# A planner that keeps pairs of PSUM banks exclusive and allows more time for transfers, and an output product that no longer begins with its direct part

## The chip, the cores and the metric

One NeuronCore of a Trainium2 chip runs the whole kernel. TensorE (PE) does matmuls, VectorE (DVE) and ScalarE (ACT) do element-wise work, SyncE (SP) issues the loads, GpSimd (POOL) issues most stores. The metric is the device time of one execution in microseconds (us); lower is better. Times below are of single executions or the median of several.

## What is computed

Input `x` has 2048 rows (sequence) and 1024 columns. The reference, cut to what matters:

```
a = x @ Wd_re.T ;  b = x @ Wd_im.T              # hidden DFT,   1024 x 1024 each
A = Ws_re @ a - Ws_im @ b                       # sequence DFT, 2048 x 2048 each, real part
h = relu(x @ w1 + b1) ** 2                      # 1024 -> 3584
B = h @ w2 + b2                                 # 3584 -> 1024
g = sigmoid((x * gate_w).sum(-1, keepdims=True))
out = g * A + (1 - g) * B
```

All of it is float32.

## The kernel before

**Precision.** A float32 operand is split into `hi` (the value rounded to fp32r by a ScalarE copy) and `lo` (the rest, a VectorE subtraction). Each product of two 128-row blocks is three matmuls into the same PSUM bank: hi x hi, hi x lo, lo x hi. For narrow operands `hi` and `lo` lie side by side in one block called `both`.

**Stages.** Four stages follow each other without a gap between them: x (the hidden DFT, results `ab`), c (the sequence DFT, results `y`, multiplied by the gate and kept in DRAM as `gy`), h (the first layer in two parts of 2048 and 1536 columns, results `h`), o (the second layer, results `o`). Each stage is a matrix product cut into 2 x 2 quarters and done in seven products in place of eight, from sums and differences of the quarters (the tables `SUMS_L`, `SUMS_R`, `FACTORS`). `seven` runs these in a given order, 1 2 5 6 3 7 4, and says which result each product is added to. A product is either *direct* (`direct`) or is itself cut once more into seven (`twice`, with quarter products 1 6 7 5 2 4 3). In stage o the products are 512 x 1792 by 1792 x 1024, the inner dimension cut into seven steps of 256; `TWICE_O = {1: 2, 2: 3, 3: 3, 4: 3}` says how many pairs of such steps go the second way. Product 4 has three pairs, and one step is left over, done directly. `FIRST_O` says for which products the left-over step comes first: its results are put into new blocks, on top of which the split part is then added; for the others it comes last, after the quarter products.

**Groups and PSUM.** A `Group` is one run of accumulation. It takes one or two of four *pairs of PSUM banks* (a tile `ps` of two rows of 512 columns, one bank each). Row r of the group goes to `ps[r // 2][:, r % 2, :]`. A group that adds to an earlier result starts with a ScalarE copy of that result into PSUM (`onto`; in the profile `ps<-u` or `ps<-o`). When a pair is done, a function takes it up: `put` and `add` write `u`, `o`, `h`, `y` or `ab` blocks, and `final` in stage o does, for each of the two rows, `(ps + b2) * (1 - g)` on VectorE, then adds `gy` (loaded as `raw`) and stores the result from POOL's queue. The last group of the kernel is taken up row by row by `last`, with one pair per row, and stored from the queues of SP and ScalarE.

**The planner.** Nothing is issued while this is recorded. Each instruction becomes an `Op` with the ops it must come after: `Queue.record` compares the parts (`box`) of blocks that they read and write. `plan` then makes the order. Matmuls stand in recorded order and have ideal times `MM` apart; every other op gets a due time backwards from them. A list scheduler with these constants runs through the program: VectorE and ScalarE by size (`VEC`, `ACT`, with ends `VEC_END`, `ACT_END`), DMA issue (`ISSUE`), a latency before and after a transfer (`RING`), a rate (`RATE`) that concurrent queues share in `flow`. On each engine the ready op that is due first goes next. The 55 blocks of 4 KB per partition (`SLOTS`) are handed out in the order of due time less a lead (`LEAD`), by kind: `raw` for loads, `out` for what reads PSUM, `hi` for the rest. `emit` writes the instructions in that order, and each engine keeps it. The framework adds the semaphore waits; those are by what is really used, not by the planner's constants.

Since one line in `emit` issues everything, all instructions of the profile have line L1125, and they are told apart by their tiles.

Of the kernel before, what the change touches and what calls it, by code (L numbers as in the profile page):

```python
# [15 lines left out]
P = 128  # L16
# [2 lines left out]
SLOTS = 55  # L19
WIDE, TALL_C, TALL_O = ((1, 2, 5, 6, 3, 7, 4),) * 3  # L20
TWICE_X, TWICE_C, TWICE_O = (1, 2, 5, 3, 4), {1: 1, 2: 4, 3: 4, 4: 4}, {1: 2, 2: 3, 3: 3, 4: 3}
FIRST_C, FIRST_O = (2,), (2, 4)
WARM = 44
FAR_TALL, FAR_WIDE = ("T2",), ()
TWICE_H = (1, 2, 5, 3, 4), (1, 2, 5, 3, 4)

MM, MM_END, FIRST_MM = 0.2267, 0.18, 6.2
VEC, VEC_END, ACT, ACT_END = (0.086, 1.0417e-3), 0.39, (0.11, 0.89e-3), 0.36
ISSUE, RING, RATE, SEM, LANES = {"sync": 0.36, "scalar": 0.36, "gpsimd": 0.56}, (1.1, 1.1), 400e3, 0.06, 8
LEAD = {"raw": 5.0, "hi": 5.0, "sum": 5.0, "out": 0.0}  # L30

ADD, SUB = ALU.add, ALU.subtract

# [11 lines left out]
def gated_mix_kernel(ctx: ExitStack, tc: tile.TileContext, x4, xn, w4, ct, w1a, w1b, w2, b1, b2, gw, out):  # L45
# [11 lines left out]
    class Sight:  # L57


        def __init__(self, base, chain, box):  # L60
            self.base, self.chain, self.box = base, chain, box
# [12 lines left out]
        def __getattr__(self, name):  # L74
            def later(*args, **kwargs):
                return Sight(self.base, self.chain + (lambda t: getattr(t, name)(*args, **kwargs),), self.box)
            return later
# [21 lines left out]
    class Op:  # L99


        def __init__(self, engine, name, args, kwargs):
            self.engine, self.name, self.args, self.kwargs = engine, name, args, kwargs
            sights = [a for a in (*args, *kwargs.values()) if isinstance(a, Sight)]
            outs = [a for a in (args[0], kwargs.get("accum_out")) if isinstance(a, Sight)]
            self.ins, self.outs = [a for a in sights if not any(a is o for o in outs)], outs
            n = max([a.size() for a in sights] + [0])
            self.load, self.end = 0.0, 0.0
            if name == "dma_start":
                self.time, self.load = ISSUE[engine], n * P * 4 / RATE  # L110
            elif engine == "tensor":
                self.time, self.end = (MM, MM_END) if n >= 512 else (0.13, 0.1)
            elif engine == "scalar":
                self.time, self.end = ACT[0] + ACT[1] * n + (1.3 if args[2] == AF.Sigmoid else 0.0), ACT_END
            elif name == "tensor_scalar":
                self.time, self.end = VEC[0] + VEC[1] * n / 2, VEC_END
            else:
                self.time, self.end = VEC[0] + VEC[1] * n, VEC_END
            self.after, self.then, self.new, self.latest, self.landed = set(), [], [], None, False
# [3 lines left out]
    class Queue:  # L123
# [5 lines left out]
        def __getattr__(self, name):  # L129
            def record(*args, **kwargs):  # L130
                op = Op(self.engine, name, args, kwargs)
                op.latest = urgent[0]
                for sight, write in [(a, False) for a in op.ins] + [(a, True) for a in op.outs]:
                    block = sight.base
                    if not block.seen and block.home in ("slot", "bank"):
                        op.new.append(block)
                    if not block.seen and block.before is not None:
                        op.after.update(o for o, *_ in block.before.seen)
                    for other, box, wrote in block.seen:
                        if (write or wrote or block.home == "bank") and (not box or not sight.box or (  # L140
                                box[0] < sight.box[1] and sight.box[0] < box[1] and (
                                    block.home == "bank" or box[2] < sight.box[3] and sight.box[2] < box[3]))):
                            op.after.add(other)
                    block.seen.append((op, sight.box, write))
                op.after.discard(op)
                ops.append(op)
                return op
            return record
# [168 lines left out]
    class Half:  # L317
# [6 lines left out]
        hi = property(lambda self: self.base.hi[:, :, self.at:self.at + 256])  # L324
# [509 lines left out]
    def c_stage():  # L834
        rows = [Row(n, False) for n in range(2)]
        to = {}

        def target(i, n, k):
            near = Near("y")
            to[near] = i, n, *k  # L840
            return near

        def final(dst, ps):
            i, n, c, rp = to[dst]
            nc.vector.tensor_tensor(dst.slot, dst.slot if ps is None else ps, rows[n].of(c).broadcast_to([P, 2, 512]),
                                    op=ALU.mult)
            rows[n].used()
            stores.append((gy[i, n, c, rp], dst, 0, 2))

        at = len(steps)  # L850
        tall(lambda i, j, q: ab[j, q, i], lambda j, n, q, c: ct[n, c, j, q], 8, TALL_C, TWICE_C, FIRST_C, target, final)
        return at, rows
# [52 lines left out]
    at, rows = c_stage()  # L905
# [5 lines left out]
    at, rows, fetched, ends = o_stage()  # L911
# [31 lines left out]
    ideal, t = [], FIRST_MM  # L943
# [10 lines left out]
    for k, (st, mv, group, also) in enumerate(steps):  # L954
# [13 lines left out]
        mv.used()  # L968
        store_all()
    emit(tc, plan(ops, len(slots), ideal[0]), slots, pools)  # L970


def plan(ops, count, start):

    t = start
# [20 lines left out]
    def lead(op, block):  # L996
        kind = "raw" if op.load else "out" if any(a.base.home == "bank" for a in op.ins) else "hi"
        return op.due - LEAD[kind]

# [10 lines left out]
    moving, at, version = {}, 0.0, 0  # L1010
    lanes = [], []

    def push(t, *what):
        heappush(events, (t, len(events) + 1e-9 * len(order), id(what), what))
# [5 lines left out]
    def loosen(op):  # L1020
        op.wait -= 1
        if not op.wait:
            able(op)

    def hand_out():
        nonlocal head
        while head < len(queue) and free:
# [2 lines left out]
            head += 1  # L1030
            loosen(op)

    def flow(t):
        nonlocal at, version
        for e in moving:
            moving[e][1] -= (t - at) / len(moving)
        at = t
        version += 1
        for e in [e for e in moving if moving[e][1] <= 1e-9]:
            op = moving.pop(e)[0]  # L1040
            push(t + RING[1], "done", op)
        for e, r in rings.items():
            if e not in moving and r:
                op = r.popleft()
                moving[e] = [op, op.load]
        if moving:
            push(t + max(0.0, min(m[1] for m in moving.values())) * len(moving), "flow", version)

    def finish(op):
        op.landed = True  # L1050
# [42 lines left out]
    while events:  # L1093
        now, _, _, what = heappop(events)
        if what[0] == "done":
            finish(what[1])
        elif what[0] == "idle" and not what[1].load:
            for o in what[1].then:
                if o.engine == what[1].engine:
                    loosen(o)  # L1100
        elif what[0] == "ring":
            rings[what[1].engine].append(what[1])
            flow(now)
        elif what[0] == "flow" and what[1] == version:
            flow(now)
        issue(now)
# [60 lines left out]
```

## Time and profile before

| what | value |
|---|---|
| median of 3 runs | 1872.18 us (1870.84 to 1874.9) |
| the profiled execution | 1871.76 us, its span 1869.6 us |
| granted TensorE clock | 0.999 |
| TensorE busy | 1852.4 us (99%), 8162 matmuls |
| VectorE busy | 1761.1 us (94%) |
| ScalarE busy | 1086.2 us (58%) |
| POOL busy | 87.6 us (5%) |
| DMA traffic | 445.04 MB, 238 GB/s over the span |
| a load of 512 KB from issue to landing, median by source | 4.5 to 12.4 us, most 5.5 to 7.3 us |

Rows of the timeline give the start in us from the span's start, the length, engine, line, instruction, `out<-in` by tile names and shape; the bracket at the end is the idle time of the engine just before, and what ended it. An engine name with a q (SPq, ACTq) is its queue, which issues DMAs. Matmuls overlap, so a matmul's length (0.39 us) is more than its step from start to start.

### The profile page before, as it was taken

The page shows a single profiled execution, that of the slowest core. Times are in us where ns is not written, and L with a number is a line of the kernel's source. Part 1 is how long each engine was busy: PE and PEld are TensorE (multiplying, and loading weights), DVE is VectorE, ACT ScalarE, POOL GpSimd, SP SyncE. Part 2 cuts the span into 40 slices and gives each one's busy share as a digit, 9 for nine tenths or more (in the row PEclk, how much of TensorE's full clock was granted, in tenths as well). Part 3 has the DMA queues.
Part 4 walks back from the last instruction along what each step waited for, and adds up shares of the span by engine and source line. Part 5 has one row for each costly group of instructions (what it writes and reads, how often), then busy time and mean ns, then how long its engine had stood idle before and what let it go on. Part 6 is the DMA issues. An engine that isn't in the chain of part 4 may idle for free. (4 is left out here: it accounts for less than half of the span.)

```text
span 1869.6 us, 22164 instructions
## 1 busy us (share of the span) xinstructions
PE 1852.4 (99%) x8162; PEld 1529.5 (82%) x8162; DVE 1761.1 (94%) x1728; ACT 1086.2 (58%) x1231; POOL 87.6 (5%) x162
## 2 busy tenths in 40 slices
PE   9999999999999999999999999999999999999998
PEld 7888888888888888888888888788887888887887
DVE  8997998999889899999997999999999998989988
ACT  6474554563343554466584798767977435364462
POOL 0000100000000000000000001000010000000000
PEclk9999999999999999999999999999999999999999
DMA  4641979449798379444551845737664798649952
GB/s 180 259 169 67 352 264 385 159 152 409 266 324 324 136 268 411 158 166 168 219 198 56 333 170 184 270 122 284 240 240 172 288 386 317 269 146 380 363 180 90
DMA packets 128860, 445.04 MB, mean 238 GB/s; under 512 B 14176, under 2 KB 23664, under 8 KB 128752
## 3 DMA queue, kind: packets, MB, share of 16 engines
q1 hardware_dynamic: 106848, 365.10, 53.1%
q0 software_dynamic: 21616, 78.14, 10.6%
q8 instruction: 64, 1.05, 0.2%
q10 hardware_dynamic: 288, 0.39, 0.1%
q14 instruction: 44, 0.36, 0.1%
HBM read 364.92 MB, written 78.65 MB: 237 GB/s over the span
## 5 line engine op out<-in xcount | busy, mean ns | idle before, releaser
L1125 PE MATMUL ps<-hi 128*128 128x512 f32 x2034 | 793.5, 391 | 6.5 <-DVE h L1125 2.6
L1125 PE MATMUL ps<-hi,lo 128*128 128x512 f32 x2034 | 792.9, 390 | 1.7 <-DVE o L1125 1.7
L1125 PE MATMUL ps<-lo,hi 128*128 128x512 f32 x2034 | 792.4, 390 | 0.0
L1125 ACT ACTIVATE hi<-raw 128x1024 fp32r<-128x1024 f32 (+2 forms) x384 | 394.2, 1037 | 341.7 <-DVE raw L1125 212.1
L1125 DVE TENSOR_TENSOR lo<-raw,hi 128x1024 fp32r<-128x1024 f32 (+2 forms) x384 | 454.1, 1200 | 13.4 <-ACT hi L1125 10.7
L1125 PEld LDWEIGHTS ps<-hi 128*128 128x128 f32 x2034 | 382.5, 188 | 88.9 <-ACT hi L1125 4.0
L1125 PEld LDWEIGHTS ps<-hi,lo 128*128 128x128 f32 x2034 | 382.5, 188 | 82.7 <-DVE o L1125 2.6
L1125 PEld LDWEIGHTS ps<-lo,hi 128*128 128x128 f32 x2034 | 382.5, 188 | 79.5 <-DVE lo L1125 0.2
L1125 PE MATMUL ps<-hi,both 128*128 128x512 f32 x1344 | 416.1, 390 | 2.5 <-ACT ps L1125 2.5
L1125 DVE TENSOR_TENSOR raw<-raw 128x1024 f32<-128x1024 f32 (+1 forms) x276 | 327.6, 1209 | 28.1 <-DMA raw<-in_ct 11.7
L1125 ACT ACTIVATE hi<-sum 128x1024 fp32r<-128x1024 f32 x216 | 219.6, 1034 | 157.5 <-DVE sum L1125 111.0
L1125 PEld LDWEIGHTS ps<-hi,both 128*128 128x128 f32 x1344 | 252.3, 188 | 56.1 <-ACT ps L1125 3.8
L1125 DVE TENSOR_TENSOR lo<-sum,hi 128x1024 fp32r<-128x1024 f32 (+1 forms) x216 | 255.1, 1198 | 13.5 <-PE ps L1125 7.4
L1125 PE MATMUL ps<-lo,both 128*128 128x512 f32 x672 | 261.7, 389 | 0.0
L1125 DVE TENSOR_TENSOR sum<-raw 128x1024 f32<-128x1024 f32 (+2 forms) x156 | 160.9, 1041 | 8.3 <-PE ps L1125 4.4
L1125 ACT ACTIVATE u<-ps 128x1024 f32<-128x1024 f32 (+1 forms) x116 | 112.2, 972 | 71.4 <-PE ps L1125 53.6
L1125 PEld LDWEIGHTS ps<-lo,both 128*128 128x128 f32 x672 | 126.2, 188 | 26.0
L1125 DVE TENSOR_TENSOR sum<-raw,sum 128x1024 f32<-128x1024 f32 (+2 forms) x117 | 128.7, 1103 | 7.2 <-PE ps L1125 6.1
L1125 DVE TENSOR_TENSOR h<-h,ps 128x1024 f32<-128x1024 f32 (+1 forms) x92 | 98.7, 1085 | 8.7 <-ACT u L1125 6.2
L1125 ACT ACTIVATE ps<-u 128x1024 f32<-128x1024 f32 (+1 forms) x84 | 82.1, 980 | 29.2 <-DVE o L1125 7.4
L1125 ACT ACTIVATE both<-sum 128x512 fp32r<-128x512 f32 x96 | 59.3, 626 | 66.0 <-DVE sum L1125 54.0
L1125 ACT ACTIVATE h<-h,b1c 128x512 f32<-128x512 f32 x112 | 75.7, 710 | 10.0 <-DVE h L1125 9.9
(47 smaller groups left out, 731.5 us busy)
## 6 DMA issues: line engine op xcount, KB each, us to landing
raw<-in_ct SPq DMA_DIRECT2D x153, 512.0 KB, 6.7
raw<-h SPq DMA_DIRECT2D x134, 512.0 KB, 7.3
raw<-in_x SPq DMA_DIRECT2D x107, 512.0 KB, 5.5
raw<-in_w SPq DMA_DIRECT2D x98, 512.0 KB, 7.1
raw<-ab SPq DMA_DIRECT2D x72, 512.0 KB, 7.1
h<-h POOLq DMA_DIRECT2D x48, 512.0 KB, 5.3
raw<-in_w1a SPq DMA_DIRECT2D x36, 512.0 KB, 6.2
ab<-ab POOLq DMA_DIRECT2D x32, 512.0 KB, 7.0
```

What stands on the lines that cost most here:

```text
L1125: made = getattr(real[op.engine], op.name)(*(actual(a) for a in op.args), **{k: actual(v) for k, v in op.kwargs.items()})
```

## The change

Four things change. The order of dependences in `Queue.record`: before, two accesses to a pair of banks depend on each other if they touch the same row of the pair; after, always, reads beside reads included. The planner's costs: ScalarE's cost per element falls and its end rises; the latencies of a transfer go from 1.1 + 1.1 to 1.6 + 2.0 us; the rate is 405 GB/s for one queue alone and 370 GB/s shared by several. The lead of loads goes from 5 to 9 us. And `FIRST_O` loses product 4, the last of stage o and of the kernel: its left-over step comes at the end, so the kernel's last group is the left-over step of one quarter (12 matmuls) and no longer a quarter product of 36.

```
-FIRST_C, FIRST_O = (2,), (2, 4)
+FIRST_C, FIRST_O = (2,), (2,)
...
-VEC, VEC_END, ACT, ACT_END = (0.086, 1.0417e-3), 0.39, (0.11, 0.89e-3), 0.36
-ISSUE, RING, RATE, SEM, LANES = {"sync": 0.36, "scalar": 0.36, "gpsimd": 0.56}, (1.1, 1.1), 400e3, 0.06, 8
-LEAD = {"raw": 5.0, "hi": 5.0, "sum": 5.0, "out": 0.0}
+VEC, VEC_END, ACT, ACT_END = (0.086, 1.0417e-3), 0.39, (0.11, 0.84e-3), 0.41
+ISSUE, RING, RATE, SEM, LANES = {"sync": 0.36, "scalar": 0.36, "gpsimd": 0.56}, (1.6, 2.0), (405e3, 370e3), 0.06, 8
+LEAD = {"raw": 9.0, "hi": 5.0, "sum": 5.0, "out": 0.0}
...
-                self.time, self.load = ISSUE[engine], n * P * 4 / RATE
+                self.time, self.load = ISSUE[engine], n * P * 4 / RATE[0]
...
-                        if (write or wrote or block.home == "bank") and (not box or not sight.box or (
-                                box[0] < sight.box[1] and sight.box[0] < box[1] and (
-                                    block.home == "bank" or box[2] < sight.box[3] and sight.box[2] < box[3]))):
+                        if block.home == "bank" or (write or wrote) and (not box or not sight.box or (
+                                box[0] < sight.box[1] and sight.box[0] < box[1] and box[2] < sight.box[3]
+                                and sight.box[2] < box[3])):
...
+    def share():
+        return 1.0 if len(moving) == 1 else len(moving) * RATE[0] / RATE[1]
+
     def flow(t):
...
-            moving[e][1] -= (t - at) / len(moving)
+            moving[e][1] -= (t - at) / share()
...
-            push(t + max(0.0, min(m[1] for m in moving.values())) * len(moving), "flow", version)
+            push(t + max(0.0, min(m[1] for m in moving.values())) * share(), "flow", version)
```

In the built program, all engines but ScalarE have as many instructions as before; ScalarE has seven fewer (copies between PSUM and `o` or `u` in product 4). TensorE's order is the same up to the first matmul of product 4. On the other engines the order differs from the first microseconds on.

## The prediction

> **What bounds the kernel now.** I read the page first, then the waits of TensorE (engine, tile, what it waited for: us in total, times, longest), then the timeline around each of those waits.
>
> ```profile
> span 1869.6 us, 22164 instructions
> PE 1852.4 (99%) x8162; PEld 1529.5 (82%) x8162; DVE 1761.1 (94%) x1728; ACT 1086.2 (58%) x1231; POOL 87.6 (5%) x162
> PEclk9999999999999999999999999999999999999999
> ...
> PE ps L1125 <- DVE h L1125: 2.6, 2, 1.8
> PE ps L1125 <- ACT ps L1125: 2.5, 3, 1.4
> PE ps L1125 <- DVE o L1125: 2.5, 3, 0.8
> PE ps L1125 <- ACT hi L1125: 1.8, 2, 1.2
> PE ps L1125 <- DVE u L1125: 1.1, 1, 1.1
> PE ps L1125 <- DVE ones L1125: 1.1, 1, 1.1
> ```
>
> TensorE is the bound, at full clock, so the matmuls themselves are out of reach of this change. What can move is the 11.6 us of waits, the tail behind the last matmul, and waits that do not exist yet. The waits for `hi` and `ones` belong to the start, which keeps its first loads and matmuls. The other nine are these, with two rows that give the pace (start, length, instruction, then idle time and who ended it):
>
> ```profile
> 1704.21 0.39 PE L1125 MATMUL ps<-lo,both 128*128 128x512 f32 x1
> ...
> 1706.93 0.39 PE L1125 MATMUL ps<-lo,hi 128*128 128x512 f32 x1
> 1708.16 0.50 PE L1125 MATMUL ps<-hi,lo 128*128 128x512 f32 x1 [0.85 <-DVE o L1125]
> 1708.50 0.39 PE L1125 MATMUL ps<-hi 128*128 128x512 f32 x1
> ...
> 1711.57 0.51 PE L1125 MATMUL ps<-hi 128*128 128x512 f32 x1 [0.84 <-DVE o L1125]
> ...
> 1715.25 0.51 PE L1125 MATMUL ps<-hi,lo 128*128 128x512 f32 x1 [0.84 <-DVE o L1125]
> ```
>
> ```profile
> 1166.42 0.50 PE L1125 MATMUL ps<-hi 128*128 128x512 f32 x1 [1.11 <-DVE u L1125]
> ...
> 1197.03 0.47 PE L1125 MATMUL ps<-hi 128*128 128x512 f32 x1 [1.76 <-DVE h L1125]
> ...
> 1226.65 0.47 PE L1125 MATMUL ps<-hi 128*128 128x512 f32 x1 [0.82 <-DVE h L1125]
> ...
> 1409.08 0.50 PE L1125 MATMUL ps<-hi,both 128*128 128x512 f32 x1 [0.60 <-ACT ps L1125]
> ...
> 1413.47 0.50 PE L1125 MATMUL ps<-hi,both 128*128 128x512 f32 x1 [1.37 <-ACT ps L1125]
> ...
> 1842.16 0.50 PE L1125 MATMUL ps<-hi,both 128*128 128x512 f32 x1 [0.57 <-ACT ps L1125]
> ```
>
> From 1704.21 to 1706.93 stand 12 steps: 0.227 us each. At 1708.16 the step took 1.23 and the next one 0.34 (to 1708.50), so 1.12 us were lost where the row shows 0.85 idle. I add that 0.27 to each idle time: lost are 3 x 1.11 = 3.3 us at 1708 to 1715, 1.4 + 2.0 + 1.1 = 4.5 at 1166 to 1227, 0.9 + 1.6 = 2.5 at 1409 and 1413, 0.8 at 1842. In all 11.1 us; no planner can gain more inside the stream.
>
> **The change, part by part.** The sum is made against the profiled execution, 1871.76 us: span 1869.6 and 2.2 around it. The median of the runs, 1872.18, lies 0.4 above.
>
> *Exclusive pairs.* The waits at 1708 to 1715 are for these:
>
> ```profile
> 1707.35 0.75 DVE L1125 SCALAR_TENSOR_TENSOR o<-ps,b2c,g 128x512 f32<-128x512 f32 x1 [0.23 <-PE ps L1125]
> ...
> 1710.76 0.75 DVE L1125 SCALAR_TENSOR_TENSOR o<-ps,b2c,g 128x512 f32<-128x512 f32 x1 [0.86 <-PE ps L1125]
> ...
> 1714.44 0.75 DVE L1125 SCALAR_TENSOR_TENSOR o<-ps,b2c,g 128x512 f32<-128x512 f32 x1 [1.11 <-PE ps L1125]
> ```
>
> Each reads row 0 of a pair while matmuls of row 1 remain: the old planner put the reader between them (1, 3 and 4 matmuls of the pair stand behind it in program order). The next matmul starts 0.05 to 0.06 us after the reader ends in all three (1708.10 to 1708.16, 1711.51 to 1711.57, 1715.19 to 1715.25): the program's own wait holds it, though it writes the other bank. In the changed order no matmul of a pair stands behind such a reader, so all three waits go: -3.3. What is late next is the reader, by the remaining matmuls (at most 4 x 0.227 = 0.9), and nobody but an output store waits for it. No other instruction's dependences change but those of matmuls, which run in one fixed order anyway, so this edit does no more. The Trainium skill (PSUM — Partial Sum Buffer, in the summary of rules for kernel authors) says that a read of PSUM beside running matmuls should target a different bank. This is that case: by it the pair needs no exclusive treatment, the edit buys nothing, and the sum below would be -1.5 in place of -4.8. The trace shows the wait in this case all the same, 0.84 to 0.85 us idle each time.
>
> *ScalarE's costs and the time for transfers.* They change no instruction; they change the order on VectorE, ScalarE, POOL and SP, and which block a load gets. Loads get their block with 9 us in hand instead of 5, so they displace `hi` and `sum` blocks. Through the order I followed three places.
>
> At 1409 and 1413 the copies into PSUM were late because VectorE came late to `u`, having idled behind ScalarE:
>
> ```profile
> 1370.39 1.23 DVE L1125 TENSOR_TENSOR lo<-sum,hi 128x1024 fp32r<-128x1024 f32 x1 [2.22 <-ACT hi L1125]
> ...
> 1372.57 0.69 DVE L1125 TENSOR_TENSOR both<-sum,both 128x512 fp32r<-128x512 f32 x1 [0.94 <-ACT both L1125]
> ...
> 1368.70 0.71 ACT L1125 ACTIVATE h<-h,b1c 128x512 f32<-128x512 f32 x1
> ...
> 1370.27 0.71 ACT L1125 ACTIVATE h<-h,b1c 128x512 f32<-128x512 f32 x1
> ```
>
> Those `h` activations, nobody's need, stand some 33 places earlier in the new order. That removes part of VectorE's 2.22 + 0.94 = 3.2 us idle; I take half, 1.6, of a possible 2.5: -1.6.
>
> At 1166 to 1227 VectorE had no rest but two waits for loads, 0.85 + 1.81 = 2.7 us:
>
> ```profile
> 1165.15 1.22 DVE L1125 TENSOR_TENSOR u<-u,ps 128x1024 f32<-128x1024 f32 x1
> ...
> 1172.96 1.23 DVE L1125 TENSOR_TENSOR raw<-raw 128x1024 f32<-128x1024 f32 x1 [0.85 <-DMA raw<-in_x]
> ...
> 1177.73 1.23 DVE L1125 TENSOR_TENSOR raw<-raw 128x1024 f32<-128x1024 f32 x1 [1.81 <-DMA raw<-in_x]
> ...
> 1165.11 1.92 SPq L1125 DMA_DIRECT2D raw<-in_x  x4
> ...
> 1156.76 0.39 PE L1125 MATMUL ps<-hi,lo 128*128 128x512 f32 x1
> ```
>
> In the changed order these four loads keep their place on SP but go into blocks whose last matmul is the one at 1156.76, so they can start 8 us sooner; the second landed 7.8 us after the burst began, hence now near 1164.7. The first `raw<-raw` moves nine places forward, ahead of the `u` addition at 1165.15 that TensorE waits for. Less work stands before both by one 768-wide instruction (0.86), so VectorE reaches the load at 1165.15 - 0.86 - 1.14 = 1163.15 and waits 1.5: 0.6 worse there. Before the `h` additions at 1197 and 1227 one more instruction (1.14, or 0.86) stands. Together 2.7 - 0.6 - 1.1 = 1.0: -1.0, between -4.5 (all gone) and +9 (below).
>
> *Product 4 without its direct part first.* No matmul is added; seven ScalarE copies of about 1 us go, off the path. Its 48 direct matmuls (48 x 0.227 = 10.9 us) move from the head of the product to its end. Two things follow. First, the split operands are due 10.9 us sooner. In the windows view of tile `both`, which only the twice split products use (window, us, busy and count by engine):
>
> ```profile
> core 0: us, PE busy (x) PEld busy (x) DVE busy (x) ACT busy (x), PEclk, DMA share, GB/s
> 1716.00:1796.00 80.00, 0.00 (x0) 0.00 (x0) 3.44 (x5) 3.15 (x5) 1.00 0.78 308
> ```
>
> VectorE has made five of them before 1796 and TensorE has used none, so VectorE is ahead by more than one such step. I take 0; without that cover TensorE would stand up to 10.9. Second, the wait at 1842: the group that takes up the last quarter product was second in line and is now third, 12 matmuls or 2.7 us later against 0.57 missing: -0.8.
>
> *The tail.* Before, the last group had 36 matmuls and VectorE was idle before its two rows. Now the last four groups end 12 matmuls (2.72 us) apart, three of them with a whole final.
>
> ```profile
> 1855.04 1.40 DVE L1125 SCALAR_TENSOR_TENSOR o<-ps,b2c,g 128x512 f32<-128x512 f32 x2
> 1856.48 1.22 DVE L1125 TENSOR_TENSOR o<-o,raw 128x1024 f32<-128x1024 f32 x1
> 1857.62 1.40 DVE L1125 SCALAR_TENSOR_TENSOR o<-ps,b2c,g 128x512 f32<-128x512 f32 x2
> ...
> 1862.89 0.75 DVE L1125 SCALAR_TENSOR_TENSOR o<-ps,b2c,g 128x512 f32<-128x512 f32 x1 [2.62 <-PE ps L1125]
> 1863.68 0.69 DVE L1125 TENSOR_TENSOR o<-o,raw 128x512 f32<-128x512 f32 x1
> 1863.83 0.39 PE L1125 MATMUL ps<-hi,both 128*128 128x512 f32 x1
> 1864.29 0.74 DVE L1125 SCALAR_TENSOR_TENSOR o<-ps,b2c,g 128x512 f32<-128x512 f32 x1
> 1865.07 0.69 DVE L1125 TENSOR_TENSOR o<-o,raw 128x512 f32<-128x512 f32 x1
> 1865.79 0.35 ACTq L1125 DMA_DIRECT2D out<-o  x1
> ```
>
> A final takes 2.58 (1855.04 to 1857.62), so the third, begun 2.65 before the last matmul's end, frees VectorE 0.07 before it. Then come both rows, 2.87 (1862.89 to 1865.07, and 0.69): 2.8 us after the last matmul, where it was 1.54 (1864.22 to 1865.76). +1.3; from 0 to +2.6, one final more, if VectorE brings a backlog. The POOL store of the third final starts with the last rows and has less behind it than the last ScalarE store.
>
> *Unseen.* Much of VectorE's queue of 1,728 instructions stands in another order. A wait costs 1.24 on average (11.1 by nine); I take half a new one, +0.6.
>
> Sum: -3.3 - 1.6 - 1.0 - 0.8 + 1.3 + 0.6 = -4.8, so 1867.0 for such an execution and, with the 0.4, **1867.4** for the median.
>
> **Rivals.**
>
> *Loads at the head of the queue (slower).* If the four loads still landed near 1172.9, `u` would start behind `raw<-raw` at 1172.96 + 1.14 = 1174.10, not 1165.15: TensorE stands 9.0 us longer. With -1.0 taken out, the rest is -3.8; the kernel is slower once that wait adds 3.8, that is when they land after 1167.8. At 9.0 the time is 1877.4. For it: VectorE's instructions start in the order of its queue, and the new order puts such reads ahead. Against: the block is free 8 us sooner.
>
> *More is won.* The loads come early enough, no wait is new: -3.3 - 4.5 - 2.5 - 0.8 + 1.3 = -9.8, 1862.4. For it: VectorE and ScalarE idle before loads in many places; against: VectorE stays full from 1180 to 1227.
>
> *The waits only move.* Three new ones more, 3.7: 1871.1. For it: VectorE is 94% busy, and any order leaves some addition late.
>
> *Pairs were not the cause.* The three waits stay: 1867.4 + 3.3 = 1870.7. Against: three times a matmul starts 0.05 us after the reader. The Trainium skill's rule of the different bank, above, would have it this way.
>
> **How the numbers follow.** The forecast has 0.50 (its own range 1864.5 to 1870), loads at the head 0.11, more won 0.17, moved waits 0.13, pairs 0.04, other losses, such as `hi` and `sum` starved of blocks, 0.05. A measurement of this kernel tells about 0.2%, 3.7 us, from no change: faster is below 1868.4, slower above 1875.9. Three quarters of the forecast and all of "more" are faster, 0.55; the rest of the forecast, the moved waits and the pairs give 0.29; 0.16 is slower. The range leaves out the far half of "more" and the slower cases: 1862 to 1874.5.
>
> **What would show it.** No wait for `DVE o` between 1700 and 1720; no `DVE o` reader between matmuls of its pair. The first `raw<-raw` near 1163, waiting under 2 us, and total TensorE waits near 5 us. The last VectorE addition 2.8 us behind the last matmul. Wrong would be a wait above 3 us on an addition behind `raw<-raw`, or a `both` matmul waiting for `lo` or `both` right after product 7.

## The result

| | before | after |
|---|---|---|
| median of 9 runs each | 1872.1 us (1870.64 to 1874.9) | 1867.4 us (1867.18 to 1868.57) |
| ratio, 95% interval | 1 | 0.9975 (0.9965 to 0.9985) |
| the profiled execution | 1871.76 us, span 1869.6 | 1867.58 us, span 1865.3 |

The changed kernel is faster by 0.25%, 4.7 us, where 1867.4 was forecast. First the page of the profile after (span, busy times, clock) and its waits of TensorE, the same two views as before (the line of `emit` is L1128 in this kernel):

```profile
span 1865.3 us, 22218 instructions
PE 1850.1 (99%) x8162; PEld 1528.2 (82%) x8162; DVE 1760.2 (94%) x1728; ACT 1075.9 (58%) x1224; POOL 87.9 (5%) x162
PEclk9999999999999999999999999999999999999999
...
PE ps L1128 <- ACT hi L1128: 3.1, 2, 2.2
PE ps L1128 <- DVE h L1128: 2.6, 4, 0.9
PE ps L1128 <- DVE lo L1128: 1.3, 2, 1.1
PE ps L1128 <- DVE ones L1128: 1.1, 1, 1.1
PE ps L1128 <- DVE u L1128: 0.5, 1, 0.5
```

The shares of busy time hardly move: TensorE is still 99% busy, VectorE 94%. What to see is which names are gone. `DVE o` (2.5 us, the three readers) and `ACT ps` (2.5 us, the copies at 1409, 1413 and 1842) have no row any more; `DVE lo` is new. `ACT hi` has grown from 1.8 to 3.1 us, all of it in the start, which as a whole is only 0.2 us later. The rows with idle time on TensorE's timeline after, outside the start:

```profile
100.12 0.50 PE L1128 MATMUL ps<-hi,lo 128*128 128x512 f32 x1 [1.11 <-DVE lo L1128]
...
1139.67 0.50 PE L1128 MATMUL ps<-hi 128*128 128x512 f32 x1 [0.34 <-DVE h L1128]
...
1167.69 0.50 PE L1128 MATMUL ps<-hi 128*128 128x512 f32 x1 [0.48 <-DVE u L1128]
...
1197.45 0.47 PE L1128 MATMUL ps<-hi 128*128 128x512 f32 x1 [0.87 <-DVE h L1128]
...
1226.82 0.47 PE L1128 MATMUL ps<-hi 128*128 128x512 f32 x1 [0.56 <-DVE h L1128]
...
1350.68 0.47 PE L1128 MATMUL ps<-hi 128*128 128x512 f32 x1 [0.85 <-DVE h L1128]
```

Matmuls stand in the same order in both kernels up to product 4, so the start of the n-th matmul can be held against the start of the n-th before. The table has the lead that it gains (minus) or loses from place to place, in us. The measured rows, each rounded, come to -4.0; before rounding they come to -4.2, all that lies between the two spans (4.3 from the rounded ones):

| place (us) | forecast | measured |
|---|---|---|
| start | 0 | +0.2 |
| 98, `lo` late | | +1.2 |
| 284 | | -0.4 |
| 1136 to 1140 | | +1.0 |
| 1166 to 1227 | -1.0 | -1.7 |
| 1350 | | +0.8 |
| 1409 and 1413 | -1.6 | -2.6 |
| 1708 to 1715, the readers | -3.3 | -3.5 |
| product 4, where the wait at 1842 was | -0.8 | -0.2 (-0.9 there, +0.6 at 1825 and 1829) |
| behind the last matmul | +1.3 | +1.2 |
| unseen | +0.6 | (the four rows without a forecast: +2.6) |
| sum | -4.8 | -4.0 |

The tail on VectorE's timeline after, with the stores that follow:

```profile
1856.15 1.41 DVE L1128 SCALAR_TENSOR_TENSOR o<-ps,b2c,g 128x512 f32<-128x512 f32 x2
1857.60 1.23 DVE L1128 TENSOR_TENSOR o<-o,raw 128x1024 f32<-128x1024 f32 x1
1858.74 0.74 DVE L1128 SCALAR_TENSOR_TENSOR o<-ps,b2c,g 128x512 f32<-128x512 f32 x1
1859.24 0.72 POOL L1128 DMA_DIRECT2D out<-o  x1 [2.01 <-DVE o L1128]
1859.52 0.69 DVE L1128 TENSOR_TENSOR o<-o,raw 128x512 f32<-128x512 f32 x1
1860.13 0.74 DVE L1128 SCALAR_TENSOR_TENSOR o<-ps,b2c,g 128x512 f32<-128x512 f32 x1
1860.24 0.34 SPq L1128 DMA_DIRECT2D out<-o  x1
1860.91 0.69 DVE L1128 TENSOR_TENSOR o<-o,raw 128x512 f32<-128x512 f32 x1
1861.63 0.35 ACTq L1128 DMA_DIRECT2D out<-o  x1
```

The last matmul ended at 1858.83; VectorE has no gap from the third final on and ends at 1861.60, 2.8 us later, where it was 1.5 before.

### The profile page after: what moved, and what is told of

The parts are those of the page before. It is cut to its first block, busy times and chain, and to the rows that moved or that the text cites. A ratio compares the mean times of both kernels' runs of the same rounds, so it can differ in the third digit from the quotient of the medians.

```text
span 1865.3 us, 22218 instructions
## 1 busy us (share of the span) xinstructions
PE 1850.1 (99%) x8162; PEld 1528.2 (82%) x8162; DVE 1760.2 (94%) x1728; ACT 1075.9 (58%) x1224; POOL 87.9 (5%) x162
## 4 chain that ended last, share of the span: by engine, by line
PE 84%; ACT 7%; DVE 6%; issue 2%; DMA 1%; SPq 0%; ACTq 0%; DVEq 0%
PE ps L1128 84%; ACT h L1128 3%; ACT hi L1128 3%; DVE lo L1128 2%; DVE h L1128 1%; DVE sum L1128 1%; ACT u L1128 1%; DVE raw L1128 1%; DMA raw<-in_x 1%; ACT ps L1128 0%; DVE o L1128 0%; DMA raw<-in_w 0%; DVE ab L1128 0%; DVE u L1128 0%; SPq L1128 0%
## 5 line engine op out<-in xcount | busy, mean ns | idle before, releaser
L1128 PE MATMUL ps<-hi 128*128 128x512 f32 x2034 | 792.2, 390 | 6.3 <-ACT hi L1128 3.1
L1128 PE MATMUL ps<-hi,lo 128*128 128x512 f32 x2034 | 791.2, 389 | 1.3 <-DVE lo L1128 1.3
L1128 PE MATMUL ps<-lo,hi 128*128 128x512 f32 x2034 | 790.9, 389 | 0.0
L1128 ACT ACTIVATE hi<-raw 128x1024 fp32r<-128x1024 f32 (+2 forms) x384 | 392.7, 1035 | 322.5 <-DVE raw L1128 183.9
L1128 DVE TENSOR_TENSOR lo<-raw,hi 128x1024 fp32r<-128x1024 f32 (+2 forms) x384 | 451.7, 1195 | 15.7 <-ACT hi L1128 10.7
L1128 PEld LDWEIGHTS ps<-hi 128*128 128x128 f32 x2034 | 382.2, 188 | 88.7 <-ACT hi L1128 3.7
L1128 PEld LDWEIGHTS ps<-hi,lo 128*128 128x128 f32 x2034 | 381.9, 188 | 81.7 <-DVE lo L1128 2.2
L1128 PEld LDWEIGHTS ps<-lo,hi 128*128 128x128 f32 x2034 | 382.0, 188 | 79.6 <-DVE lo L1128 0.4
L1128 PE MATMUL ps<-hi,both 128*128 128x512 f32 x1344 | 415.2, 389 | 0.1
L1128 DVE TENSOR_TENSOR raw<-raw 128x1024 f32<-128x1024 f32 (+1 forms) x276 | 324.3, 1203 | 8.6 <-DMA raw<-in_ct 6.3
L1128 ACT ACTIVATE hi<-sum 128x1024 fp32r<-128x1024 f32 x216 | 220.7, 1034 | 180.2 <-DVE sum L1128 121.7
L1128 PEld LDWEIGHTS ps<-hi,both 128*128 128x128 f32 x1344 | 252.2, 188 | 53.2 <-DVE both L1128 0.5
L1128 DVE TENSOR_TENSOR lo<-sum,hi 128x1024 fp32r<-128x1024 f32 (+1 forms) x216 | 254.8, 1195 | 14.5 <-PE ps L1128 12.0
L1128 PE MATMUL ps<-lo,both 128*128 128x512 f32 x672 | 261.4, 389 | 0.0
L1128 DVE TENSOR_TENSOR sum<-raw 128x1024 f32<-128x1024 f32 (+2 forms) x156 | 160.8, 1038 | 17.2 <-PE ps L1128 14.7
L1128 ACT ACTIVATE u<-ps 128x1024 f32<-128x1024 f32 (+1 forms) x116 | 112.4, 972 | 79.9 <-PE ps L1128 62.4
L1128 PEld LDWEIGHTS ps<-lo,both 128*128 128x128 f32 x672 | 126.1, 188 | 26.1
L1128 DVE TENSOR_TENSOR sum<-raw,sum 128x1024 f32<-128x1024 f32 (+2 forms) x117 | 128.4, 1099 | 1.9 <-PE ps L1128 0.6
L1128 DVE TENSOR_TENSOR h<-h,ps 128x1024 f32<-128x1024 f32 (+1 forms) x92 | 98.2, 1081 | 7.4 <-ACT u L1128 5.9
L1128 ACT ACTIVATE both<-sum 128x512 fp32r<-128x512 f32 x96 | 58.7, 623 | 69.9 <-DVE sum L1128 48.9
L1128 ACT ACTIVATE ps<-u 128x1024 f32<-128x1024 f32 (+1 forms) x80 | 78.0, 977 | 23.9 <-DVE u L1128 5.8
L1128 ACT ACTIVATE h<-h,b1c 128x512 f32<-128x512 f32 x112 | 76.1, 710 | 11.2 <-DVE h L1128 11.2
```

Of the source, the lines that this page charges most:

```text
L1128: made = getattr(real[op.engine], op.name)(*(actual(a) for a in op.args), **{k: actual(v) for k, v in op.kwargs.items()})
```

## The experiments

The parts were put in and taken out one at a time. Ratios are each against runs of the kernel before beside it, so that they can be held against each other; a median is of that kernel's own runs.

| kernel | pairs | product 4 | transfers | lead 9 | ScalarE costs | median us | ratio (95%) |
|---|---|---|---|---|---|---|---|
| after | new | new | new | new | new | 1867.4 | 0.9975 (0.9965 to 0.9985) |
| e1 | new | old | old | old | old | 1868.9 | 0.9983 (0.9974 to 0.9992) |
| e2 | old | new | old | old | old | 1874.6 | 1.0012 (1.0003 to 1.0021) |
| e3 | new | old | new | new | new | 1865.6 | 0.9967 (0.9955 to 0.9979) |
| e4 | old | new | new | new | new | 1873.8 | 1.0007 (0.9999 to 1.0016) |
| e5 | new | old | new | old | old | 1863.2 | 0.9947 (0.9935 to 0.9959) |
| e6 | new | old | old | new | old | 1866.0 | 0.9962 (0.9949 to 0.9974) |
| e7 | new | old | old | old | new | 1867.3 | 0.9968 (0.9957 to 0.9980) |
| e8 | new | old | new | new | old | 1863.0 | 0.9947 (0.9933 to 0.9960) |
| e9 | new | new | new | new | old | 1864.0 | 0.9950 (0.9937 to 0.9962) |
| e10 | new | old | longer still | new | old | 1863.8 | 0.9949 (0.9936 to 0.9963) |

### Pairs and product 4

**e1**, only the dependence rule changed:

```
-                        if (write or wrote or block.home == "bank") and (not box or not sight.box or (
...
+                        if block.home == "bank" or (write or wrote) and (not box or not sight.box or (
```

> The kernel before with exclusive pairs as the only change. Theory: the three waits at 1708 to 1715 us (0.85 + 0.84 + 0.84 us idle, 3.3 us with the slow steps) come from readers placed between the matmuls of their pair; in this order no matmul of a pair stands behind such a reader, the rest of the order is the old one, so 1872.1 - 3.3 = 1868.8 us, and the other six waits stay within 0.3 us each. Rival (the pair is not the cause, the additions were just late): the waits stay, 1872.1 us.

Measured: 0.9983, 3.2 us. The three waits are gone and the lead jumps by 3.5 us at that place, as expected. The six other waits did not stay within 0.3 us: at 1166 the idle time grew from 1.11 to 1.68, at 1409 the wait of 0.60 was gone, at 1413 it fell from 1.37 to 0.85, and 0.9 us was lost at 1135 to 1138, though VectorE's order up to these places is the old one. So from one execution of the same order to another, such places differ by half a microsecond and more, 1409 and 1413 together by 1.4. The theory stands, the rival falls.

**e2**, only product 4:

```
-FIRST_C, FIRST_O = (2,), (2, 4)
+FIRST_C, FIRST_O = (2,), (2,)
```

> The kernel before with product 4 without its direct part first as the only change. Theory: in this order six readers, not three, stand between matmuls of their pair (three new ones in the last 10 us, where the left-over steps end row by row), so +3.3 us, -0.8 for the wait at 1842, +1.2 for the tail: 1872.1 + 3.7 = 1875.8 us. Rival (the two parts of the change do not need each other): +1.2 - 0.8 only, 1872.5 us.

Measured: 1.0012, 2.2 us slower, where 3.7 were expected and the rival had 0.4. On TensorE's timeline of e2 near its end:

```profile
1853.97 0.50 PE L1125 MATMUL ps<-hi,lo 128*128 128x512 f32 x1 [0.84 <-DVE o L1125]
...
1858.10 0.50 PE L1125 MATMUL ps<-hi 128*128 128x512 f32 x1 [0.84 <-DVE o L1125]
...
1862.00 0.50 PE L1125 MATMUL ps<-hi 128*128 128x512 f32 x1 [0.84 <-DVE o L1125]
```

The three new waits are there, each exactly as long as those at 1708 to 1715. The wait at 1842 is gone. What is missing is 0.7 us of the tail (5.9 us behind the last matmul, not 6.5: the waits space the last finals out, so VectorE has no queue there) and a net 1.2 us that this execution gained ahead of product 4, 1.7 of it won at 1409 and 1413, where nothing had been changed.

**e3**, the changed kernel with the old `FIRST_O`:

> The changed kernel with the direct part of product 4 first again. Theory: the new order of product 4 cost more than it gave: the tail behind the last matmul goes from 6.5 back to 5.3 us (-1.2), the short waits at 1825 and 1829 (0.6 lost) go, the wait at 1842 (0.8) may return: 1867.4 - 1.0 = 1866.4 us. Rival (the new order of product 4 is part of the gain): 1867.4 + 0.8 or more, 1868.2 us and above.

Measured: 0.9967 in place of 0.9975. The intervals overlap, so by the times alone it is no proof; the profiles show the place. From before product 4 (where e3 leads by 6.5 us and the changed kernel by 5.1) to the last matmul e3 loses 0.3 and the changed kernel wins 0.2, but behind the last matmul it is 4.95 against 6.50 us. The rest of the 2.4 us between their spans, 1.4 us, arose ahead of product 4, 1.3 of it within the first 15 us, where two executions differ in their first loads. e8 and e9 below also differ in product 4 alone and say the same: e8 loses 0.3 and e9 wins 0.2 up to the last matmul, and behind it they take 4.94 and 6.49 us. So in both pairs of profiles the new product 4 costs 1.0 us.

**e4**, the changed kernel with the old dependence rule:

> The changed kernel without exclusive pairs. Theory: six readers stand between matmuls of their pair, each makes the next matmul wait 1.1 us with its slow step: 1867.4 + 6.7 = 1874.1 us, with six waits for DVE o of 0.8 us idle. Rival (with the new costs of ScalarE and of transfers the readers come late enough anyway): 1867.4 us.

Measured: 1.0007 in place of 0.9975, 6.0 us, with six waits for `DVE o`, 5.1 us idle in all:

```profile
PE ps L1128 <- DVE o L1128: 5.1, 6, 0.8
```

So the rule for pairs is worth 3.2 us to the old kernel and 6.0 to the new one: without it the three readers that the new product 4 adds cost 3.5 us on TensorE's timeline.

### The planner's costs

**e5**, **e6**, **e7**: each on top of e1. The edits are the lines of the diff for `RING`, `RATE` and `share` (e5), for `LEAD` (e6), for `ACT` and `ACT_END` (e7).

> Exclusive pairs and, of the costs, the transfer latencies and rates alone (lead 5, old ScalarE costs, product 4 as before); to be held against exclusive pairs alone, 1868.9 us. Pairs with all three costs took 1865.6, so 3.3 us are to be shared out. Theory (loads that start earlier take away VectorE's waits for loads and with them TensorE's waits at 1165 to 1227 and 1409): loads become startable 0.6 to 1.2 us earlier against their use, about a third of what all three give, so -1 us, 1867.9; VectorE's waits for loads fall from 30 us to about 23. Rival (any reshuffle gives about a microsecond either way): 1867.9 to 1869.9 with no relation to the waits for loads.

> Exclusive pairs and the lead of 9 us for loads alone; against 1868.9. Theory: loads become startable 2 to 2.7 us earlier, most of what all three give, so -2.2 us, 1866.7; VectorE's waits for loads fall from 30 us to about 15. At 1197 to 1227 two more VectorE instructions stand ahead of the h additions, which can cost 1 us. Rival (reshuffle): 1867.9 to 1869.9.

> Exclusive pairs and the new ScalarE costs alone; against 1868.9. Theory: no load starts earlier, so the waits for loads stay near 30 us and the time is 1868.9 within 0.8 us. Rival (reshuffle): as much as the other two, 1867.9 to 1869.9; or all of the 3.3 us if ScalarE's order was the cause of the waits at 1409: 1866.

Measured: e5 0.9947, e6 0.9962, e7 0.9968, against 0.9983 of e1. The waits of VectorE for transfers (loads, in e6 also 3.2 us for stores), summed over their rows, are 33.1 us before, 29.9 in e1, 22.0 in e5, 23.0 in e6, 28.6 in e7, 10.5 in the changed kernel. That half of the theory holds for e5 and e7, where it forecast 23 and 30; for e6 it forecast 15. The other half does not hold: e5 wins far more than its share, and e6 less than e5 though both shorten the waits alike. The rival does no better, since all three medians lie below its 1867.9. So the sum of the waits for loads does not tell the time; single places do, where the order of a queue has changed. The lead of matmul n over the kernel before, in profiled executions, names the places:

| place (us) | e1 | e5 | e6 | e7 | after |
|---|---|---|---|---|---|
| 98 | 0.0 | 0.0 | 0.0 | +1.1 | +1.2 |
| 1135 to 1140 | +0.9 | 0.0 | 0.0 | +0.7 | +1.0 |
| 1166 to 1227 | +0.2 | -1.6 | -0.8 | -0.9 | -1.7 |
| 1350 | 0.0 | 0.0 | 0.0 | +1.1 | +0.8 |
| 1409 and 1413 | -1.4 | -2.6 | -0.5 | -2.6 | -2.6 |

At 1409 and 1413 the question is why ScalarE keeps VectorE waiting. The prediction named four `h` activations that nobody needs. In the built orders of the kernel before, e1 and e6 they stand at places 941 to 951 of ScalarE's queue, around the `hi` copy that VectorE waits for (944); in e7 and in the changed kernel all four, in e5 three of them, stand at 908 to 917. VectorE's timeline in e6:

```profile
1368.28 1.22 DVE L1125 TENSOR_TENSOR lo<-sum,hi 128x1024 fp32r<-128x1024 f32 x1 [1.38 <-ACT hi L1125]
...
1370.46 0.69 DVE L1125 TENSOR_TENSOR both<-sum,both 128x512 fp32r<-128x512 f32 x1 [0.95 <-ACT both L1125]
```

and the same two instructions in the changed kernel, with no idle time ahead of them:

```profile
1369.05 1.22 DVE L1128 TENSOR_TENSOR lo<-sum,hi 128x1024 fp32r<-128x1024 f32 x1
1370.19 0.69 DVE L1128 TENSOR_TENSOR both<-sum,both 128x512 fp32r<-128x512 f32 x1
```

But in e8 and e9 (below) the four stand at 943 to 951 again, around the same copy, and TensorE does not wait. What the four kernels with a wait share is another row of ScalarE, two or three instructions ahead of that copy: a `hi<-raw` that waits for a store of `h` to land. ScalarE's timeline before, and in e8 (the last row of each cut is the copy):

```profile
1366.79 1.06 ACT L1125 ACTIVATE hi<-raw 128x1024 fp32r<-128x1024 f32 x1 [2.41 <-DMA h<-h]
1367.76 1.04 ACT L1125 ACTIVATE hi<-sum 128x1024 fp32r<-128x1024 f32 x1
1368.70 0.71 ACT L1125 ACTIVATE h<-h,b1c 128x512 f32<-128x512 f32 x1
1369.32 1.05 ACT L1125 ACTIVATE hi<-sum 128x1024 fp32r<-128x1024 f32 x1
```

```profile
1359.86 1.06 ACT L1128 ACTIVATE hi<-raw 128x1024 fp32r<-128x1024 f32 x1
1360.83 1.04 ACT L1128 ACTIVATE hi<-sum 128x1024 fp32r<-128x1024 f32 x1
1361.78 0.71 ACT L1128 ACTIVATE h<-h,b1c 128x512 f32<-128x512 f32 x1
1362.39 1.05 ACT L1128 ACTIVATE hi<-sum 128x1024 fp32r<-128x1024 f32 x1
```

This wait is 2.41 us before, 1.74 in e1, 1.41 in e2, 2.19 in e6; of the other eight kernels only e9 has it (1.21 us, ended at 1361.31), and there VectorE idles 0.18 us behind it. So the activations in their old place do no harm without that wait. Whether moving them away would be enough while the wait stays, no run shows. The wait also differs between executions: e1 and e2, with VectorE's old order up to here, lose 1.2 and 0.9 us at 1409 and 1413 where the profiled execution of the kernel before lost 2.6.

TensorE then waits 1.76 us at 1411.69 in e6, 0.85 at 1412.70 in e1, 0.60 at 1412.34 in e2, and not at all in the changed kernel, e3 to e5 and e7 to e10.

The waits at 98 and 1350 are there in the kernels with the new ScalarE costs and in no other. That is why e7 wins little by its profile (span 1865.8 against 1865.4 in e1): it gains 1.2 us more than e1 at 1409 and loses 2.2 at 98 and 1350.

**e8**, the first two costs together, and **e9**, the changed kernel with the old ScalarE costs:

```
-VEC, VEC_END, ACT, ACT_END = (0.086, 1.0417e-3), 0.39, (0.11, 0.84e-3), 0.41
+VEC, VEC_END, ACT, ACT_END = (0.086, 1.0417e-3), 0.39, (0.11, 0.89e-3), 0.36
```

> Exclusive pairs, transfer costs and lead, without the new ScalarE costs; against 1865.6 for all three. Theory: loads start as early as with all three, so 1865.6 within 0.8 us, and VectorE's waits for loads stay near 11 us. Rival (the ScalarE costs carry a part): 1866.6 or more.

> The changed kernel with the old ScalarE costs. Theory: the new ScalarE costs put one VectorE addition ahead at 98 and one at 1350 us, each makes TensorE wait about 0.9 to 1.1 us idle (those waits are there in all kernels with the new costs, and in none without); without them 1867.4 - 2.2 = 1865.2 us, and no wait for DVE lo at 98. Rival (they came with the longer transfers or the lead): 1867.4.

Measured: e8 0.9947 where all three costs gave 0.9967 (e3), so leaving the ScalarE costs out wins 3.7 us more by the ratios, 2.2 by the spans (the intervals overlap a little); neither theory nor rival had that sign. e9 was made to test it on the whole change: 0.9950 in place of 0.9975, 4.7 us by the ratios, 3.2 by the spans (1862.1 against 1865.3), where 2.2 were expected. Its waits of TensorE:

```profile
PE ps L1128 <- ACT hi L1128: 3.1, 2, 2.3
PE ps L1128 <- DVE h L1128: 1.5, 2, 0.9
PE ps L1128 <- DVE ones L1128: 1.1, 1, 1.1
PE ps L1128 <- DVE lo L1128: 0.2, 1, 0.2
```

The 1.1 us for `DVE lo` are gone and two of four `DVE h`. The mechanism at 98 is the place of one VectorE addition some 20 us earlier. In the changed kernel and in e8:

```profile
79.56 1.22 DVE L1128 TENSOR_TENSOR ab<-ab,ps 128x1024 f32<-128x1024 f32 x1
80.69 1.22 DVE L1128 TENSOR_TENSOR sum<-raw 128x1024 f32<-128x1024 f32 x1
...
97.71 3.49 DVE L1128 TENSOR_TENSOR lo<-sum,hi 128x1024 fp32r<-128x1024 f32 x3
```

```profile
76.71 2.35 DVE L1128 TENSOR_TENSOR sum<-raw 128x1024 f32<-128x1024 f32 x2
79.19 1.22 DVE L1128 TENSOR_TENSOR ab<-ab,ps 128x1024 f32<-128x1024 f32 x1
...
96.21 3.49 DVE L1128 TENSOR_TENSOR lo<-sum,hi 128x1024 fp32r<-128x1024 f32 x3
```

The `ab` addition reads a result of TensorE and starts at the same point of the matmul stream in both (which runs 0.37 us later in the changed kernel). With the new costs one of the two `sum<-raw` stands behind it, without them both stand ahead. So from there to the `lo` instructions that TensorE needs, VectorE takes 18.15 us in place of 17.02, one addition more. All four kernels with the new costs have the first order, the other eight the second. What puts VectorE late at 1350 was not followed in this way. The wait at 1136 to 1140 is not explained so: e1 has it too, without the new costs and with the old order; in e9 it is gone as well, which is 1.0 of the 3.2 us between the spans.

**e10**, e8 with still longer transfers:

```
-(1.6, 2.0), (405e3, 370e3)
+(2.2, 3.0), (405e3, 370e3)
```

> Exclusive pairs, lead 9, old ScalarE costs, product 4 as before, and the latencies of a transfer raised once more, from 1.6 + 2.0 to 2.2 + 3.0 us; against 0.9947 of the kernel before with 1.6 + 2.0. Theory (the gain of the longer transfers is that loads start early enough): VectorE's waits for loads are down to 10 us already and TensorE waits for none of them, so more gives nothing: the ratio stays within 0.0005 of 0.9947, waits for loads 5 to 10 us. Rival (each microsecond of planned latency gives): 2 us less, ratio 0.9936.

Measured: 0.9949, as the theory had it. VectorE's waits for loads are down to 4.5 us, a little below the 5 to 10 expected:

```profile
DVE raw L1128 <- DMA raw<-in_ct: 2.4, 2, 1.5
DVE sum L1128 <- DMA raw<-in_x: 2.1, 1, 2.1
```

and TensorE gets nothing from it. e5, e8 and e10 are level, and all three are faster than both kernels of the change: exclusive pairs and longer transfers, with the old product 4 and the old ScalarE costs.

## Why the prediction was right

*The three waits* were right in place, cause and size: -3.3 forecast, -3.5 at that place in the profiles of the changed kernel and of e1, and 3.2 for e1 as a whole. e4 says more: six such readers in the changed kernel, six waits of 0.84. The rival that the pair was not the cause has fallen, and with it the reading of the different-bank rule as a reason against the change. The Trainium skill (PSUM — Partial Sum Buffer, summary of rules for kernel authors) has a read beside running matmuls target a different bank. These reads do, and no run here shows a clash; but the read at 1707.35 waited for TensorE and the matmul at 1708.16 for the read, so in this program the waits are by the pair.

*1409 and 1413*: right in place, and in that VectorE idled behind ScalarE; what held ScalarE up was read only in part. The prediction named the `h` activations and not the 2.41 us that ScalarE waits for a store just ahead of them, and e8 shows that with the activations in their old place and no such wait nothing is lost. The idle time behind ScalarE went wholly, not by half; both waits are gone, -2.6. But e1 and e2, with VectorE's old order, lose only 1.2 and 0.9 there: part of the -2.6 is the one execution that was profiled, and the 1.6 of the forecast lies within what executions of the old order lose.

*1166 to 1227*: the balance was right in sign, -1.0 against -1.7. Not right was the load that VectorE would meet at 1163 and wait 1.5 us for. The timeline of SP's queue after, where the burst starts, and that of VectorE, which comes to the first of its loads:

```profile
1158.85 1.77 SPq L1128 DMA_DIRECT2D raw<-in_x  x4
```

```profile
1165.28 1.22 DVE L1128 TENSOR_TENSOR raw<-raw 128x1024 f32<-128x1024 f32 x1
1166.42 1.81 DVE L1128 TENSOR_TENSOR u<-u,ps 128x1024 f32<-128x1024 f32 x2
1168.15 1.22 DVE L1128 TENSOR_TENSOR lo<-sum,hi 128x1024 fp32r<-128x1024 f32 x1
```

The burst began 6.3 us sooner than before (not 8: the whole stream ran 1.9 us late at that place, from the new waits at 98 and 1140), and VectorE came to it at 1165.28 for the same reason, with no wait. So the first two loads had landed within 6.4 us of the start of the burst; the prediction had kept the 7.8 of the kernel before. The rival of loads at the head of the queue did not happen.

*1842*: the wait is gone as forecast, but 0.6 us came back at 1825 and 1829, where the prediction saw none: net -0.2 for -0.8.

*The tail*: +1.3 forecast, +1.2 measured, the last addition 2.8 us behind the last matmul as worked out.

*Unseen* was the term that was mis-sized: half a new wait, +0.6, was allowed for. The four places without a forecast come to +2.6. Two of them, at 98 and 1350, have a cause, the ScalarE costs, to which the prediction gave no term of its own; it had counted them only for their good effect at 1409. The error was in part balanced by the two places where it had been too careful. Profile against profile, 1867.0 was forecast and 1867.58 measured; that the median came out as 1867.4 to the digit is luck. One of the signs that the prediction named did not come: TensorE's waits were to be near 5 us in total and are 8.6, of which 4.4 are in the start.

## What to carry to other kernels

When instructions are placed by a planner, its idea of what excludes what has to match the waits that the framework really adds; where the planner is more liberal, it puts readers where they stop the engine that bounds the kernel, and the waits show as equal idle times (here 0.84 us, every time). One edit can need another: the new end of product 4 costs 2.2 us without the pair rule. With the rule it still costs 1.0 us by the profiles, so the change would have been better without it. A constant closer to the measured time need not give the better order: for a 1024-wide instruction of ScalarE the new costs plan 0.97 us (0.11 + 0.84 x 1.024) and the old 1.02; on the timeline before, two such copies in a row start 0.95 apart (1145.66 and 1146.61), and yet the old ones were better by 2 to 5 us (e8 against e3, e9 against the changed kernel, by spans and by ratios): in a queue with no slack the place of a single instruction decides.

## What was not expected

The waits are equal: 15 of 15 readers between matmuls of their pair, in three kernels, gave 0.84 or 0.85 us of idle time. The waits of TensorE at 1409 and 1413 began with a store, some 45 us earlier: ScalarE waited for its landing, and VectorE for ScalarE. And VectorE's waits for loads, 33 us before, could be cut to 4.5 us with no gain in time over e5, which still has 22: those last 17 us were not on TensorE's path, though VectorE is 95% busy.
